# Second expert layer of a fused attention and mixture-of-experts kernel: loop order of the four row tiles and the three split terms

## The chip, the cores and the metric

The kernel runs on one core of a Trainium2 chip. The metric is device time in microseconds (us) of the whole launch; the time before is a median of three runs. One more execution was taken with the hardware profiler, and every statement on where time goes comes from that one.

TensorE multiplies a stationary operand (128 x 128, loaded by its own weight-load instruction) with a moving operand and adds the result into a region of PSUM, the accumulator memory. ScalarE (ACT), VectorE (DVE) and GpSimd (POOL) work beside it, each from its own queue in order; SyncE (SP) issues most DMA transfers.

## The reference

Two stages in fp32. The first is an attention over channels, for each of 4 batches of 5056 tokens with 256 channels; the second sends each of the 20224 resulting rows through one of 8 experts, chosen by the largest gate logit.

```python
qn = q / (norm(q, axis=1) + 1e-6); kn = k / (norm(k, axis=1) + 1e-6)
a = softmax(kn.T @ qn / tau)              # 256 x 256 per batch
x = (v @ a).reshape(20224, 256)
logits = x @ w_gate + modality_bias[modality_id]
e = argmax(logits); gate_w = softmax(logits)[e]
out = gate_w * (relu(x @ w1[e]) @ w2[e])  # w1[e]: 256 x 1024, w2[e]: 1024 x 256
```

## The kernel before, in words

**Split products.** TensorE's fp32r form is used for speed, and each operand is split into a high part (rounded to fp32r) and a low part (the rest). A product of two fp32 matrices then takes three terms: high times high, high times low, low times high. In names, `h` at the end is the high part and `l` the low one: `w2h`, `w2l`, `hh`, `hl`.

**Stages.** A first stretch builds the 256 x 256 Gram matrices (`g`, L343) of the batches from `q` and `k`, 512 tokens a step. After a softmax, `v` is transposed (`vtp`, L521), multiplied with the attention and gate weights (`xp`, L539), routed, and its rows are scattered by expert into a DRAM buffer `xs`. As soon as 512 rows of one expert stand there, a block can run. There are 40 blocks: 38 of four row tiles of 128 rows, and the last two of three tiles. Work on later batches (`g`, `vtp`, `xp`) is interleaved with the blocks until about 1080 us; after that only blocks remain.

**One block** (`block_pieces`). SP loads the expert's weights and the rows; ACT and DVE split the weights (L722, L729) and TensorE transposes the rows. For each of eight slices j of the 1024 hidden units:

- `m1(j)`: six products of 512 columns (384 in a three-tile block) into one PSUM tile `hp`; then ACT makes `hh` = relu (L765) and DVE `hl`, what is left of it (L766).
- `m2(j)`: the second layer. For each row tile t, three products of 256 columns each into the tile's accumulator region: `hh*w2h`, `hh*w2l`, `hl*w2h`. The stationary operand is the slice of `hh` or `hl` for row tile t, the moving one 256 columns of `w2h` or `w2l`. Twelve products a slice, 96 a block of four tiles.

The four accumulator regions lie in two PSUM tiles: `y0` holds row tiles 0 and 1, `y1` holds 2 and 3. There is one copy of each, so the next block can write them only when they have been read. After the eighth slice, `finish(t)` lets ACT copy region t, scaled with the gate weight, to `yo` (L796), and POOL scatters those rows to the output (L454).

**Order.** `m2(j)` is emitted two slices behind `m1(j)`. Around the end of a block the order is: first layer slice 0 of the next block, `m2(6)`, first layer slice 1 of the next, `m2(7)`, the four copies, first layer slice 2 of the next, then `m2(0)` of the next, which writes `y0` and `y1` again. A scheduler in the tile layer puts the emitted instructions into the engines' queues and may move ready ones ahead; on the chip each queue runs in the order in which it then stands. A reader of PSUM waits for the last write to the tile (here `y0` or `y1`), not to a region of it. In the last block the last three slices are emitted one row tile at a time.

Of the kernel before, what the change touches and what calls it, by code (L numbers as in the profile page):

```python
# [34 lines left out]
def kernel(  # L35
# [14 lines left out]
    P = 128  # L50
# [390 lines left out]
    def order(ins, others):  # L441

        for other in others:
            tc.add_manual_dep(
                ins, other.name,
                mybir.DependencyInfo(mybir.DependencyClass.NoSync, mybir.DependencyReason.DATA),
                reason="order on a queue",
            )
# [224 lines left out]
    def block_pieces(g, slot, picked, tail):  # L673
        pki, padded = picked
        st = {"wr": {}, "wc": {}, "h": {}}
# [95 lines left out]
        def m2(j, ts=range(tt)):  # L771
            if j == 0:
                st["y"] = [ps1.tile([P, 2, D], F32, tag=f"y{i}", name=f"y{i}_{slot}") for i in range(2)]
            _, _, w2h, w2l = st["wc"][j // 2]
            hh, hl = st["h"][j]
            for t in ts:
                y = st["y"][t // 2][:, t % 2, :]
                tsl = slice(t * P, (t + 1) * P)
                for i, (a, w) in enumerate(((hh, w2h), (hh, w2l), (hl, w2h))):
                    ins = nc.tensor.matmul(  # L780
                        y, a[:, tsl], w[:, j % 2, :],
                        start=(j == 0 and i == 0 and t % 2 == 0), stop=(j == NJ - 1 and i == 2),
                        skip_group_check=True,
                    ).ins
                    if slot == NB_MIN - 1 and j >= NJ - 3:

                        if t > 0:
                            order(ins, st["prev"][t - 1])
                        st.setdefault("prev", {}).setdefault(t, []).append(ins)
# [23 lines left out]
        for j in range(1, NJ):  # L813
            body.append(lambda j=j: m1(j))
            if j % 2 == 1 and (j + 1) // 2 + 1 < NJ // 2:
                body.append(lambda j=j: split_w((j + 1) // 2 + 1))
            if j >= BEHIND and (not ending or j - BEHIND < NJ - 3):
                body.append(lambda j=j: m2(j - BEHIND))
        if ending:

            last = []
            for t in range(tt):
                last += [lambda j=j, t=t: m2(j, range(t, t + 1)) for j in range(NJ - 3, NJ)]
                last.append(lambda t=t: finish(t))
        else:
            last = [lambda j=j: m2(j) for j in range(NJ - BEHIND, NJ)]
            last += [lambda t=t: finish(t) for t in range(tt)]
# [170 lines left out]
```

## Time and profile before

| what | value |
|---|---|
| median of three runs | 1247.93 us (1247.73 to 1249.01) |
| the profiled execution | 1241.93 us, span 1240.2 us |
| granted TensorE clock | 0.997 |
| TensorE matmuls | 1215.5 us busy, 98% of the span, 8368 |
| of these, second layer (L780) | 3 x 1264 products |
| VectorE / ScalarE / GpSimd busy | 67% / 59% / 29% |

In a row of the profile `y<-w2h,hh` means: writes `y`, reads moving `w2h` and stationary `hh`. `x1264` is a count, and after the bar come the busy time in us and the mean of one in ns. The busy time of one product is the time from its start to its end; successive products overlap, so the step from one start to the next is shorter than that.

### The profile page before, as it was taken

Reading aid. Unit: us, or ns where it says so; the run is one execution under the profiler, and the core shown is the slowest. Engines: PE = TensorE matmul, PEld = TensorE weight load, DVE = VectorE, ACT = ScalarE, POOL = GpSimd, SP = SyncE. Lnnn points to the kernel's source line nnn. Section 1 sums busy time; section 2 is a strip of 40 time slices with the busy share of each in tenths; the row PEclk is TensorE's granted clock in tenths of the full one; section 3 lists DMA queues with packets and bytes.
Section 4 is the critical chain, followed back from the end, with each engine's and each line's share of the span. In section 5 each row is a group of like instructions: output and inputs, shape, how many; then the busy total and the mean of one; then the engine's idle time right before and its main releaser. Section 6 shows DMA issues by size and latency. Waiting matters only on the chain. (4 is left out here: it accounts for less than half of the span.)

```text
span 1240.2 us, 23781 instructions
## 1 busy us (share of the span) xinstructions
PE 1215.5 (98%) x8368; PEld 1116.8 (90%) x8368; DVE 829.3 (67%) x2182; ACT 736.7 (59%) x1511; POOL 365.1 (29%) x344
## 2 busy tenths in 40 slices
PE   8989999999999999999999999999999999999997
PEld 7878898999999999998999999999899999989997
DVE  6789687767667776776677776656555665575552
ACT  6656667766666666675666666556455555545552
POOL 0053342223232333312333323322322233333121
PEclk9999999999999999999999999999999999999999
DMA  8979565455555565545555554444554454443430
GB/s 309 297 236 298 161 200 174 156 171 177 185 184 171 172 182 184 178 143 165 178 181 188 154 185 152 147 131 138 174 165 137 148 162 149 126 145 123 147 98 29
DMA packets 104177, 210.83 MB, mean 170 GB/s; under 512 B 11336, under 2 KB 52808, under 8 KB 104048
## 3 DMA queue, kind: packets, MB, share of 16 engines
q1 hardware_dynamic: 88304, 167.61, 43.5%
q0 software_dynamic: 15744, 41.61, 9.0%
q8 instruction: 67, 1.10, 0.4%
q14 instruction: 62, 0.51, 0.1%
HBM read 167.06 MB, written 43.43 MB: 170 GB/s over the span
## 5 line engine op out<-in xcount | busy, mean ns | idle before, releaser
L454 POOL DMA_INDIRECT xs<-x,pi x160 | 179.5, 1122 | 681.5 <-ACT w1h L722 302.3
L780 PE MATMUL y<-w2h,hh 128*128 128x256 f32 x1264 | 357.6, 283 | 1.8 <-issue 0.9
L780 PE MATMUL y<-w2l,hh 128*128 128x256 f32 x1264 | 352.6, 279 | 0.1
L780 PE MATMUL y<-w2h,hl 128*128 128x256 f32 x1264 | 350.9, 278 | 0.1
L766 DVE SCALAR_TENSOR_TENSOR hl<-hp,hh 128x512 fp32r<-128x512 f32 (+1 forms) x320 | 216.4, 676 | 67.8 <-ACT hh L765 61.4
L762 PE MATMUL hp<-xh,w1h 128*128 128x512 f32 (+1 forms) x640 | 254.4, 398 | 0.0
L762 PE MATMUL hp<-xh,w1l 128*128 128x512 f32 (+1 forms) x640 | 250.3, 391 | 0.0
L762 PE MATMUL hp<-xl,w1h 128*128 128x512 f32 (+1 forms) x640 | 249.9, 391 | 0.0
L780 PEld LDWEIGHTS y<-w2h,hh 128*128 128x128 f32 x1264 | 237.5, 188 | 13.1 <-ACT yo L796 1.9
L780 PEld LDWEIGHTS y<-w2l,hh 128*128 128x128 f32 x1264 | 238.0, 188 | 10.1 <-issue 0.5
L765 ACT ACTIVATE hh<-hp 128x512 fp32r<-128x512 f32 (+1 forms) x320 | 190.3, 595 | 82.6 <-PE hp L762 75.7
L780 PEld LDWEIGHTS y<-w2h,hl 128*128 128x128 f32 x1264 | 236.7, 187 | 0.5 <-DVE hl L766 0.3
L729 DVE TENSOR_TENSOR w1l<-w1r,w1h 128x512 fp32r<-128x512 f32 x160 | 110.2, 689 | 179.4 <-ACT w1h L722 171.3
L454 POOL DMA_INDIRECT out_dram<-yo,xr x158 | 171.7, 1087 | 158.0 <-ACT yo L796 121.4
L722 ACT CAST w1h<-w1r 128x512 fp32r<-128x512 f32 x160 | 100.1, 626 | 142.9 <-PE hp L762 130.1
L762 PEld LDWEIGHTS hp<-xh,w1l 128*128 128x128 f32 x640 | 120.1, 188 | 26.0
L762 PEld LDWEIGHTS hp<-xl,w1h 128*128 128x128 f32 x640 | 120.4, 188 | 14.7 <-issue 0.4
L762 PEld LDWEIGHTS hp<-xh,w1h 128*128 128x128 f32 x640 | 120.1, 188 | 12.7
L722 ACT CAST w2h<-w2r 128x512 fp32r<-128x512 f32 x160 | 101.0, 631 | 48.4 <-PE y L780 45.8
L729 DVE TENSOR_TENSOR w2l<-w2r,w2h 128x512 fp32r<-128x512 f32 x160 | 110.2, 689 | 25.3 <-ACT w2h L722 23.2
L543 ACT COPY x<-xp 128x264 f32<-128x264 f32 x160 | 61.2, 383 | 91.2 <-PE xp L539 67.5
L539 PE MATMUL xp<-ah,vh 128*128 128x264 f32 x320 | 93.1, 291 | 0.4 <-issue 0.4
(146 smaller groups left out, 1710.4 us busy)
## 6 DMA issues: line engine op xcount, KB each, us to landing
w1r<-in_moe_w_dram SPq DMA_DIRECT2D x80, 512.0 KB
w2r<-in_moe_w_dram SPq DMA_DIRECT2D x80, 512.0 KB
xr<-xs SPq DMA_DIRECT2D x38, 516.0 KB
v<-in_v_dram SPq DMA_DIRECT2D x36, 512.0 KB
q<-in_q_dram SPq DMA_DIRECT2D x35, 512.0 KB
k<-in_k_dram SPq DMA_DIRECT2D x35, 512.0 KB
xs<-x,pi POOLq DMA_INDIRECT x160
out_dram<-yo,xr POOLq DMA_INDIRECT x158
```

Of the source, the lines that this page charges most:

```text
L454: ins = nc.gpsimd.indirect_dma_start(out=dst, out_offset=bass.IndirectOffsetOnAxis(ap=idx, axis=0), in_=rows, in_offset=None, bounds_check ...
L539: nc.tensor.matmul(xp[:, 0:DE], a[:, h, t * P : (t + 1) * P], w[:, h, :], start=i == 0, stop=i == len(seq) - 1,)
L543: nc.scalar.copy(st["x"][:, t, :], xp[:, 0:DE])
L722: ins = nc.scalar.copy(hi, src).ins
L729: nc.vector.tensor_tensor(lo, src, hi.bitcast(F32), ALU.subtract)
L762: nc.tensor.matmul(hp[:, 0:rows], w[:, h, fs], x[:, h, 0:rows], start=i == 0, stop=i == len(seq) - 1)
L765: nc.scalar.activation(hh[:, 0:rows], hp[:, 0:rows], AF.Relu)
L766: nc.vector.scalar_tensor_tensor(hl[:, 0:rows], hp[:, 0:rows], 0.0, hh[:, 0:rows].bitcast(F32), ALU.max, ALU.subtract)
L780: ins = nc.tensor.matmul(y, a[:, tsl], w[:, j % 2, :], start=(j == 0 and i == 0 and t % 2 == 0), stop=(j == NJ - 1 and i == 2), skip_group ...
```

## The change

In `m2` the loop over the three terms goes outside, and the loop over the row tiles inside. The same twelve products are issued, with the same operands and into the same four regions. Before, three successive products went to one region. Now each goes to another region than the one ahead of it: `hh*w2h` for tiles 0, 1, 2, 3, then `hh*w2l` for all four, then `hl*w2h` for all four. The start flag (first slice, first term, tiles 0 and 2) and the stop flag are those of before. Where `m2` is called for a single tile (the last three slices of the last block) the order stays. Line numbers behind L780 move up by two; L780 is L778 in the changed kernel, L796 is L794.

```diff
-            for t in ts:
-                y = st["y"][t // 2][:, t % 2, :]
-                tsl = slice(t * P, (t + 1) * P)
-                for i, (a, w) in enumerate(((hh, w2h), (hh, w2l), (hl, w2h))):
+            for i, (a, w) in enumerate(((hh, w2h), (hh, w2l), (hl, w2h))):
+                for t in ts:
                     ins = nc.tensor.matmul(
-                        y, a[:, tsl], w[:, j % 2, :],
+                        st["y"][t // 2][:, t % 2, :], a[:, t * P : (t + 1) * P], w[:, j % 2, :],
                         start=(j == 0 and i == 0 and t % 2 == 0), stop=(j == NJ - 1 and i == 2),
                         skip_group_check=True,
                     ).ins
```

TensorE's queue, last slice of block 35 (`y0_35` and `y1_35` are its two accumulator tiles). Before:

```order
L780 MATMUL y0_35_16314<-w2h_35_3_16343,hh_35_7_16467 128x256 [waits Activation_49]
L780 MATMUL y0_35_16314<-w2l_35_3_16344,hh_35_7_16467 128x256
L780 MATMUL y0_35_16314<-w2h_35_3_16343,hl_35_7_16468 128x256
L780 MATMUL y0_35_16314<-w2h_35_3_16343,hh_35_7_16467 128x256
L780 MATMUL y0_35_16314<-w2l_35_3_16344,hh_35_7_16467 128x256
L780 MATMUL y0_35_16314<-w2h_35_3_16343,hl_35_7_16468 128x256
L780 MATMUL y1_35_16315<-w2h_35_3_16343,hh_35_7_16467 128x256
```

Five more rows on `y1` follow it. In the changed kernel the slice reads:

```order
L778 MATMUL y0_35_16314<-w2h_35_3_16343,hh_35_7_16467 128x256 [waits Activation_49]
L778 MATMUL y0_35_16314<-w2h_35_3_16343,hh_35_7_16467 128x256
L778 MATMUL y1_35_16315<-w2h_35_3_16343,hh_35_7_16467 128x256 x2
L778 MATMUL y0_35_16314<-w2l_35_3_16344,hh_35_7_16467 128x256 x2
L778 MATMUL y1_35_16315<-w2l_35_3_16344,hh_35_7_16467 128x256 x2
L778 MATMUL y0_35_16314<-w2h_35_3_16343,hl_35_7_16468 128x256 x2
L778 MATMUL y1_35_16315<-w2h_35_3_16343,hl_35_7_16468 128x256 x2
```

The last write to `y0` was the sixth product of the slice and is now the tenth; that to `y1` stays the twelfth. The first write to `y1`, which in the next block's first slice waits for ACT's copies, was the seventh and is now the third.

ACT's queue at the end of block 4, one of those in the mixed stretch, as a difference:

```order
 L765 ACTIVATE hh_5_1_3632<-hp_5_1_3625 128x512
-L796 ACTIVATE yo_4_3652<-y0_4_3259,xr_4_2608 128x256 x2
-L796 ACTIVATE yo_4_3652<-y1_4_3260,xr_4_2608 128x256 x2
+L322 ACTIVATE sq_2_3_0_k_4552<-k_2_3_4505 128x512
+L794 ACTIVATE yo_4_3652<-y0_4_3259,xr_4_2608 128x256 x2
 L525 CAST vh_12_3621<-vtp_12_0_3657 128x512
+L794 ACTIVATE yo_4_3652<-y1_4_3260,xr_4_2608 128x256 x2
 L525 CAST vh_12_3621<-vtp_12_1_3688 128x512
 L722 CAST w2h_5_3_3751<-w2r_5_1_3089 128x512
-L322 ACTIVATE sq_2_3_0_k_4552<-k_2_3_4505 128x512
```

The scheduler puts a square (`sq`) ahead of the copies and a cast of `vh` between the two pairs of copies. In the stretch with blocks alone (block 35, for one) ACT's order is unchanged.

## The prediction

> **What bounds the kernel now.** I read the page's busy times first, then the stretches, then the waits. The question was whether TensorE waits for anybody or is itself the limit.
>
> ```profile
> span 1240.2 us, 23781 instructions
> PE 1215.5 (98%) x8368; PEld 1116.8 (90%) x8368; DVE 829.3 (67%) x2182; ACT 736.7 (59%) x1511; POOL 365.1 (29%) x344
> L780 PE MATMUL y<-w2h,hh 128*128 128x256 f32 x1264 | 357.6, 283 | 1.8 <-issue 0.9
> L780 PE MATMUL y<-w2l,hh 128*128 128x256 f32 x1264 | 352.6, 279 | 0.1
> L780 PE MATMUL y<-w2h,hl 128*128 128x256 f32 x1264 | 350.9, 278 | 0.1
> ```
>
> TensorE is busy for 98% of the span, the next engine for 67%. The second layer is 3792 products, and the idle time ahead of its three rows is 1.8, 0.1 and 0.1 us. Only two things can therefore move the time: how fast TensorE steps from product to product, and new waits. The stretches and TensorE's waits, from the views that group them:
>
> ```profile
> 600.00:900.00 300.00, 299.42 (x2108) 276.43 (x2107) 199.66 (x523) 178.41 (x366) 91.09 (x84) 1.00 0.51 160
> 1080.00:1232.00 152.00, 151.13 (x1027) 140.35 (x1026) 82.33 (x195) 75.43 (x151) 42.97 (x42) 1.00 0.35 110
> PE y L780 <- ACT yo L796: 0.8, 2, 0.6
> PEld y L780 <- ACT yo L796: 1.9, 3, 0.8
> PEld y L780 <- DVE hl L766: 0.3, 1, 0.3
> ```
>
> TensorE is full both in the mixed stretch (299.42 of 300 us) and in the one with blocks alone (151.13 of 152), at a granted clock of 1.00, so the clock has no room to rise. The waits of the second layer are on ACT's copies `yo`, 0.8 us and 1.9 us, and 0.3 us on `hl`. The chain of waits is of no help here: it ends on POOL and "issue" and names no TensorE work.
>
> **The change part by part. First part: the step.** Nothing is added: 3792 products and as many weight loads stay. What may change is the step. These are starts on TensorE in the last slice of block 35 and around it, ACT's four copies, and below them durations over the whole run (minimum, median, maximum):
>
> ```profile
> 1152.34 0.28 PE L780 MATMUL y<-w2h,hh 128*128 128x256 f32 x1
> ...
> 1152.94 0.28 PE L780 MATMUL y<-w2h,hl 128*128 128x256 f32 x1
> 1153.06 0.28 PE L780 MATMUL y<-w2h,hh 128*128 128x256 f32 x1
> ...
> 1153.40 0.28 PE L780 MATMUL y<-w2h,hh 128*128 128x256 f32 x1
> 1153.52 0.28 PE L780 MATMUL y<-w2l,hh 128*128 128x256 f32 x1
> 1153.64 0.27 PE L780 MATMUL y<-w2h,hl 128*128 128x256 f32 x1
> 1153.75 0.39 PE L762 MATMUL hp<-xh,w1h 128*128 128x512 f32 x1
> ...
> 1155.13 0.28 PE L780 MATMUL y<-w2h,hh 128*128 128x256 f32 x1
> ...
> 1155.36 0.28 PE L780 MATMUL y<-w2h,hl 128*128 128x256 f32 x1
> ```
>
> ```profile
> L780 PE MATMUL y<-w2h,hh x1264: 277/279/388, 99.6 to 1232.1; 128*128 128x256 f32 x181
> L780 PE MATMUL y<-w2l,hh x1264: 277/277/387, 99.8 to 1232.2; 128*128 128x256 f32 x181
> L780 PE MATMUL y<-w2h,hl x1264: 274/276/386, 102.7 to 1232.4; 128*128 128x256 f32 x181
> L796 ACT ACTIVATE yo<-y,xr x158: 459/476/513, 129.2 to 1232.7; 128x256 f32<-128x256 f32 x158
> ```
>
> ```profile
> 1153.33 1.56 ACT L796 ACTIVATE yo<-y,xr 128x256 f32<-128x256 f32 x4
> ```
>
> The twelve products take 1153.75 - 1152.34 = 1.41 us, 117.5 ns each. A duration of 279 ns holds that step and about 160 ns in which the next product already runs, so I read differences of durations as differences of steps. By the medians, `hh*w2h` is the slowest (279), then `hh*w2l` (277), then `hl*w2h` (276); by the means 283, 279, 278.
>
> The fast one is the last of its row tile: the product behind it goes to another region. The two slower ones are followed by a product into the region that they have just written. There is a cleaner comparison: during `hl*w2h` of one tile and `hh*w2h` of the next, TensorE streams the same `w2h` and loads the same weights, `hh` of the next tile, for the product behind it. They differ in the part held in the array, in whether the successor uses the same moving operand, and in whether it writes the same region. Now every product inside a term has a successor with the same moving operand and another region, like the fast row. So the nearest row says that all three settle at the third row's value: by medians (279-276) + (277-276) = 4 ns per row tile and slice, times 1264 = 5.1 us; by means (283-278) + (279-278) = 6 ns, 7.6 us. The mean of the first row holds a few waits, so I take 6 us between the two.
>
> The bounds of this term: all three at the least that the third row shows, 274: (5 + 3 + 2) x 1264 = 12.6 us saved. On the other side stands the Gram row, where successive products also change region, after every third one:
>
> ```profile
> L343 PE MATMUL g<-qs,ks 128*128 128x256 f32 (+1 forms) x600 | 81.8, 283 | 1.3 <-issue 1.3
> ```
>
> These are split products of 256 columns too, and they average 283 ns. If all second-layer products went to 283, against 283 + 279 + 278 = 840 now, 9 ns x 1264 = 11.4 us would be added. I take the value near the first end because it comes from the same operands.
>
> **Second part: the copies at the block's end.** In the rows above, `y0` is last written by the sixth product (1152.94, ends 1153.22), and ACT starts its four copies at 1153.33, 0.11 us later. It runs them back to back and ends at 1153.33 + 1.56 = 1154.89. Now the last write to `y0` is the tenth product, four steps later: 4 x 0.1175 = 0.47 us. The copies start near 1153.80 and end near 1155.36. The next block's first slice starts at 1155.13. Before, `y1` was wanted by its seventh product, now by its third, at 1155.36, with the weight load some 0.1 us ahead of that. So here TensorE waits some 0.15 us where it waited for nothing. Behind the copies in ACT's queue stand the cast of `w2h` and relu of the next first-layer slice; they too come up to 0.47 us late, but that relu's `hh` is wanted only after four more slices of about 1.4 us, which hide it.
>
> With a three-tile block behind, the first layer between is shorter:
>
> ```profile
> 1198.43 1.56 ACT L796 ACTIVATE yo<-y,xr 128x256 f32<-128x256 f32 x4
> 1199.96 0.28 PE L780 MATMUL y<-w2h,hh 128*128 128x256 f32 x1
> ...
> 1200.19 0.28 PE L780 MATMUL y<-w2h,hl 128*128 128x256 f32 x1
> ```
>
> Copies would end at 1199.99 + 0.47 = 1200.46, and `y1` is wanted at 1200.19 less 0.1: 0.35 to 0.4 us. By the timeline, only the first layer's six products stand between at eight of the 39 block ends: six like block 35 (6 x 0.15 = 0.9 us) and two with a three-tile block (2 x 0.4 = 0.8 us). Two more have ACT late already, as here, where TensorE waited for `y0`:
>
> ```profile
> 1108.99 0.39 PE L780 MATMUL y<-w2h,hh 128*128 128x256 f32 x1 [0.21 <-ACT yo L796]
> ```
>
> There `y1` comes four steps sooner, 2 x 0.4 = 0.8 us. The other 29 have transposes or `xp` products between, which cover the copies and the cast that the scheduler puts among them:
>
> ```profile
> 684.14 1.03 PE L521 MATMUL vtp<-ident,v 128*128 128x128 f32 x8
> 684.93 0.48 PE L762 MATMUL hp<-xh,w1h 128*128 128x512 f32 x1
> ```
>
> The transposes give 684.93 - 684.14 = 0.8 us more. Were that cover gone, each end could cost the full 0.47 us, 29 x 0.47 = 13.6 us. Bounds of this part: 0, and 2.5 + 13.6 = 16.1 us; I take 0.9 + 0.8 + 0.8 = 2.5 us.
>
> **Third part.** `hl` is wanted as the ninth product instead of the third, which can save the 0.3 us in the row above and no more. The last three slices of the last block stand as they stood, so the end of the kernel, with POOL's stores, is unchanged.
>
> **Sum:** -6 + 2.5 - 0.3 = -3.8 us. The profiled execution took 1241.93 us around its span of 1240.2, and the median is 6.0 us above that. I carry the difference over to the median: 1247.93 - 3.8 = **1244.1 us**.
>
> **The rivals.** Changes under 0.2%, 2.5 us, cannot be told from none.
>
> *The step does not depend on the region.* Then only the waits are left: 1247.93 + 2.2 = 1250.1 us. For it: the Gram row changes region every third product and is no faster; the order 279, 277, 276 may belong to the operands themselves. Against it: the comparison above, in which streamed and loaded operands are the same.
>
> A rule for this rival, by itself: the Trainium skill, "TensorE: Matmul & The Clock Gate", section "Back-to-back issue gap", gives the step at full clock as N/2.4 + 2.5 ns, an estimate of 109 ns for 256 columns, with no term for the accumulator. The trace has 117.5 ns, so something that the rule leaves out costs time here, and the rule does not say whether the change touches it. By that rule the first part would be nothing.
>
> *The step gets longer,* to the Gram row's mean: +11.4 + 2.2 gives 1261.5 us. For it: fresh weights at every product, where before the second of three loaded the slice that the array already held. Against it: the weight loads are as many as before, and the third row, which is followed by fresh weights, is the fast one.
>
> *The copies turn into a wait at every block end.* One mechanism: four products later on ACT, four sooner on TensorE. It decides once the last copy ends later than 0.23 us behind the first product of the next block. With the gain on the step kept this is 1247.93 - 6 + 16.1 = 1258.0 us. For it: the rows of blocks 35 and 37 are already there. Against it: 0.8 us of transposes or the like at most other ends.
>
> **How the numbers follow.** Forecast 0.42, with a range of its own from 1236 to 1248; step unchanged 0.28; step longer 0.18; copies everywhere 0.12. Faster by over 0.2%: nine tenths of the forecast and a little of the second case, 0.40. Within 0.2%: the rest of the forecast, about 0.04, most of the second case, 0.20, and 0.03 from mild forms of the others: 0.27. Slower: 0.33. The range reaches from 1236, the first bound less the waits (1247.93 - 12.6 + 0.5), to 1258, where the copies' case stands and about half of the longer-step case is left out.
>
> **What would show it.** If the step depends on the region, the L778 rows all fall to 276 ns or less and to nearly one value, and a slice takes under 1.39 us; if the operands decide it, the order 279, 277, 276 stays; if fresh weights cost, the first two rows rise above 280. The copies should start four steps later in block 35, and the wait of `y` for `yo` should rise from 0.8 + 1.9 us by some 2.5 us; 10 us or more there would mean the last rival. The forecast is wrong if TensorE's busy time does not fall by about 6 us.

## The result and the profile after

The changed kernel takes 1264.15 us, the median of four runs (1263.23 to 1266.07), against 1248.46 us for four runs of the kernel before on the same chip. The ratio is 1.0124, with a 95% interval of 1.011 to 1.0137: 15.7 us slower. Forecast were 1244.1 us and a range of 1236 to 1258. In two later sets of runs the ratio was 1.0159 and 1.0174. The profiled execution of the changed kernel has a span of 1262.5 us, 22.3 us more than before.

The changed kernel's page, its groups and its waits (the numbers in a row of waits are us in all, times, and the longest one in us):

```profile
span 1262.5 us, 23777 instructions
PE 1227.7 (97%) x8368; PEld 1126.0 (89%) x8368; DVE 832.5 (66%) x2182; ACT 736.7 (58%) x1511; POOL 359.3 (28%) x344
L778 PE MATMUL y<-w2h,hh 128*128 128x256 f32 x1264 | 211.6, 285 | 13.8 <-ACT yo L794 13.4 <-issue 0.2
L778 PE MATMUL y<-w2h,hl 128*128 128x256 f32 x1264 | 203.4, 282 | 0.1
L778 PE MATMUL y<-w2l,hh 128*128 128x256 f32 x1264 | 202.1, 279 | 0.0
PEld y L778 <- ACT yo L794: 18.7, 20, 2.6
PE y L778 <- ACT yo L794: 13.4, 15, 2.2
ACT sq_k L322 <- DMA k<-in_k_dram: 21.5, 17, 3.5
```

Two things differ. The second layer's wait for the copies `yo` rose from 0.8 to 13.4 us on the products and from 1.9 to 18.7 us on their weight loads; the two overlap, so they are not added. And `hl*w2h`, before the fastest of the three groups (278 ns), now averages 282 ns. The busy times of these rows (211.6 us where the first had 357.6) cannot be held against those of before: time in which products of one row overlap counts once, and now four of a row stand together.

Where the time goes is seen by stretches. Busy time of TensorE is the first pair behind the length, the granted clock the number behind the five pairs. Before, and then after:

```profile
300.00:400.00 100.00, 100.00 (x710) 92.61 (x709) 67.68 (x166) 61.48 (x125) 27.16 (x24) 1.00 0.50 162
```

```profile
300.00:400.00 100.00, 96.28 (x652) 88.13 (x651) 64.92 (x153) 58.70 (x119) 30.17 (x27) 0.97 0.50 161
600.00:900.00 300.00, 298.31 (x2089) 275.17 (x2089) 199.70 (x519) 177.95 (x364) 88.01 (x82) 1.00 0.51 161
```

Between 300 and 400 us TensorE issued 652 matmuls instead of 710, and its clock fell to 0.97. By the start of the last second-layer product of a block, the changed kernel is behind by 3.0 us at block 3 (227.86 against 230.81), by 13.2 us at block 7 (349.59 against 362.83), and by 22.3 us at block 38. So 3.0 us are lost up to block 3, 10.2 us in four blocks, and 9.1 us over the 31 behind them. Of the 3.0 us, 1.6 stand there already at the first second-layer product (101.24 against 99.62 us), ahead of all that the change touches. Of the 10.2 us, TensorE's waits for the copies of blocks 4, 5 and 6 make 0.71, 2.59 and 2.88 us, a lower clock 3.4 us and the step (both below) 0.4 us. Of the 9.1 us, the step makes 31 x 96 x 1.07 ns = 3.2 us and waits for copies at seven ends 4.9 us, where the kernel before has 0.2.

This is what happens in the four blocks. ACT at the end of block 6, first in the kernel before, then in the changed one; in brackets stands the idle time ahead of the row and what ended it:

```profile
318.93 0.59 ACT L765 ACTIVATE hh<-hp 128x512 fp32r<-128x512 f32 x1
319.42 1.56 ACT L796 ACTIVATE yo<-y,xr 128x256 f32<-128x256 f32 x4
320.85 1.10 ACT L525 CAST vh<-vtp 128x512 fp32r<-128x512 f32 x2
...
323.42 0.63 ACT L322 ACTIVATE sq_k<-k 128x512 f32<-128x512 f32 x1 [0.96 <-DMA k<-in_k_dram]
```

```profile
325.96 0.59 ACT L765 ACTIVATE hh<-hp 128x512 fp32r<-128x512 f32 x1
330.07 0.63 ACT L322 ACTIVATE sq_k<-k 128x512 f32<-128x512 f32 x1 [3.51 <-DMA k<-in_k_dram]
330.60 0.82 ACT L794 ACTIVATE yo<-y,xr 128x256 f32<-128x256 f32 x2
331.32 0.58 ACT L525 CAST vh<-vtp 128x512 fp32r<-128x512 f32 x1
331.78 0.86 ACT L794 ACTIVATE yo<-y,xr 128x256 f32<-128x256 f32 x2
```

ACT's waits for loads of `k` ahead of such squares are 21.5 us in all in the changed kernel; before they were:

```profile
ACT sq_k L322 <- DMA k<-in_k_dram: 15.7, 15, 3.3
```

Here the square of `k` waits for a load, and starts 4 to 4.5 us behind relu in both kernels (330.07 - 325.96 and 323.42 - 318.93). Before, the four copies ran in that time. Now the square stands ahead of them in ACT's queue, ACT idles 3.51 us with the copies behind it, and a cast parts the two pairs. TensorE at the same place:

```profile
326.40 0.63 PE L778 MATMUL y<-w2h,hl 128*128 128x256 f32 x4
...
328.91 0.40 PE L762 MATMUL hp<-xh,w1l 128*128 128x512 f32 x1
331.48 0.51 PE L778 MATMUL y<-w2h,hh 128*128 128x256 f32 x2 [2.17 <-ACT yo L794]
332.69 0.80 PE L778 MATMUL y<-w2h,hh 128*128 128x256 f32 x2 [0.71 <-ACT yo L794]
333.29 1.05 PE L778 MATMUL y<-w2l,hh 128*128 128x256 f32 x4
334.14 1.05 PE L778 MATMUL y<-w2h,hl 128*128 128x256 f32 x4
```

It waits 2.17 us for `y0`, runs two products, and waits again, 0.71 us, for `y1`. Behind that the four `w2l` products take 334.14 - 333.29 = 0.85 us instead of 0.47: the clock is down, as the stretches show (granted clock behind the five pairs).

```profile
328.00:331.00 3.00, 1.31 (x6) 0.73 (x4) 0.27 (x1) 0.93 (x3) 0.00 (x0) 1.00 0.69 217
331.00:332.00 1.00, 0.51 (x2) 0.30 (x2) 0.49 (x2) 1.00 (x4) 0.67 (x1) 0.94 0.13 53
334.00:335.00 1.00, 1.00 (x7) 1.00 (x7) 1.00 (x3) 1.00 (x3) 1.00 (x1) 0.50 0.38 131
336.00:340.00 4.00, 4.00 (x20) 3.48 (x19) 0.90 (x3) 1.50 (x3) 1.10 (x1) 0.66 0.56 192
```

The granted clock falls to 0.50 just before 332 us and is back near 338.7 (4 us at a mean of 0.66). At half speed for 6.8 us TensorE does 3.4 us less work, which is more than the wait itself.

### The profile page after: what moved, and what is told of

Read it like the earlier page. It is cut to its first block, busy times and chain, and to the rows that moved or that the text cites. A ratio compares the mean times of both kernels' runs of the same rounds, so it can differ in the third digit from the quotient of the medians.

```text
span 1262.5 us, 23777 instructions
## 1 busy us (share of the span) xinstructions
PE 1227.7 (97%) x8368; PEld 1126.0 (89%) x8368; DVE 832.5 (66%) x2182; ACT 736.7 (58%) x1511; POOL 359.3 (28%) x344
## 4 chain that ended last, share of the span: by engine, by line
PE 80%; issue 7%; DMA 4%; ACT 4%; DVE 3%; POOL 1%; POOLq 0%; SPq 0%; ACTq 0%; DVEq 0%
PE y L778 30%; PE hp L762 28%; PE xp L539 9%; PE g L343 9%; DMA k<-in_k_dram 4%; PE vtp L521 2%; PE xtp L743 2%; ACT yo L794 1%; POOL out_dram L454 1%; DMA xs<-x,pi 1%; POOL xs L454 0%; ACT hh L765 0%; PE ns L370 0%; ACT vh L525 0%; DVE qs L299 0%
## 5 line engine op out<-in xcount | busy, mean ns | idle before, releaser
L778 PE MATMUL y<-w2h,hh 128*128 128x256 f32 x1264 | 211.6, 285 | 13.8 <-ACT yo L794 13.4
L778 PEld LDWEIGHTS y<-w2h,hh 128*128 128x128 f32 x1264 | 189.7, 188 | 39.3 <-ACT yo L794 18.7
L778 PE MATMUL y<-w2h,hl 128*128 128x256 f32 x1264 | 203.4, 282 | 0.1
L778 PE MATMUL y<-w2l,hh 128*128 128x256 f32 x1264 | 202.1, 279 | 0.0
L778 PEld LDWEIGHTS y<-w2l,hh 128*128 128x128 f32 x1264 | 172.3, 188 | 0.0
L778 PEld LDWEIGHTS y<-w2h,hl 128*128 128x128 f32 x1264 | 171.2, 188 | 0.3 <-DVE hl L766 0.3
```

The lines of the kernel that those rows point to most:

```text
L778: ins = nc.tensor.matmul(st["y"][t // 2][:, t % 2, :], a[:, t * P : (t + 1) * P], w[:, j % 2, :], start=(j == 0 and i == 0 and t % 2 == 0) ...
```

## The experiments

Ratios are to the kernel before on the same chip, in the same set of runs; its medians there lay between 1233 and 1245 us. "The step" is the mean time from the start of one second-layer product to the next matmul's start, in one profiled execution, over the 3660 to 3740 steps below 135 ns; the waits in the last column are of that one execution, too. The step is 116.88 ns before and 117.95 ns after. Times 3791 steps that difference of 1.07 ns is 4.1 us.

| kernel | ratio, 95% interval | step, ns | wait of `y` products for `yo`, us |
|---|---|---|---|
| change, again | 1.0159 (1.0124 to 1.0193) | 117.96 | 11.2 |
| change, a third time | 1.0174 (1.0143 to 1.0205) | 117.92 | 10.3 |
| slices 1 to 6 only | 1.0016 (1.0000 to 1.0032) | 117.72 | 0.6 |
| last slice only | 1.0070 (1.0044 to 1.0096) | 116.88 | 6.3 |
| first slice only | 1.0003 (0.9992 to 1.0014) | 117.04 | 1.2 |
| first and last slice | 1.0145 (1.0124 to 1.0167) | 117.03 | 11.9 |
| change, ACT's old queue | 1.0023 (1.0005 to 1.0042) | 117.91 | 1.4 |
| before, ACT's new queue | 1.0055 (1.0033 to 1.0078) | 116.90 | 6.7 |
| before, five squares ahead | 1.0036 (1.0019 to 1.0053) | 116.87 | 4.4 |
| change, five squares behind | 1.0080 (1.0054 to 1.0106) | 117.89 | 3.5 |
| regions turn | 0.9991 (0.9974 to 1.0008) | 116.86 | 0.6 |
| operands turn | 1.0015 (1.0000 to 1.0030) | 117.70 | 1.5 |
| fresh weights | 0.9997 (0.9979 to 1.0015) | 116.86 | 0.8 |
| snake | 1.0004 (0.9987 to 1.0021) | 117.71 | 0.6 |
| spread | 0.9998 (0.9987 to 1.0008) | 116.85 | 0.6 |

### Which slices: the middle, and the last

The slice's twelve products are put into one list, and the change's order is taken in some slices alone. For slices 1 to 6:

```diff
+            by_term = [(i, t) for i in range(3) for t in ts]
+            by_tile = [(i, t) for t in ts for i in range(3)]
+            todo = by_term if 0 < j < NJ - 1 else by_tile
+            for i, t in todo:
```

> Terms outside only in the second-layer slices 1 to 6 of a block; the first and the last slice as before. ACT's, DVE's, SP's and POOL's queues then stand exactly as before, and only TensorE's order differs, on 6/8 of the products. If the loss came from TensorE's step alone, 6/8 of the 15.7 us show: about +12 us. If ACT's queue and the late copies are the cause, only the small rise of the step is left, read as 1.05 ns on 3791 products (116.89 to 117.94 ns) = 4.0 us in all, 6/8 of it: +3 us.

Measured: 1.0016, 2.0 us. The queues of ACT, DVE, GpSimd and SyncE are those of the kernel before, the waits for `yo` stay at their old size, and the step is 117.72 ns. So the step's part can be had alone. The time's interval just reaches no change (1.0000); that it is a loss is read from the step.

For the last slice alone the condition is `j == NJ - 1`; the queues are then exactly those of the changed kernel.

> Terms outside only in the last slice of a block, 1/8 of the products. ACT's, DVE's, SP's and POOL's queues then stand exactly as in the changed kernel. If the step is the cause: +2 us (1/8 of 15.7). If the queues and the late copies are: 15.7 less 7/8 of the step's 4.0 us, about +12 us, and waits of y for yo near the changed kernel's 13.4 us.

Measured: 1.0070, 8.9 us, at the old step of 116.88 ns: nearer to the 12 us of the second theory than to the 2 us of the first, but short of it, with 6.3 us of waits where 13.4 were named. In its trace the loss arises in blocks 3 to 8: it is 0.7 us behind the kernel before at block 2, 11.6 at block 8 and 11.5 at the end. Not all of that is waits for the copies: 3.4 us are a clock at half for 6.8 us from 218 us on, behind a wait of 3.2 us for the routing (`rp`, L575), and in three kernels that lose nothing (first slice, fresh weights, spread) the clock fell there, too, for 3.4 us. The move of `y0`'s last write by four products, with all that the scheduler makes of it, is a large part of the loss.

### ACT's queue apart from the order of the products

Every instruction of ACT is tied, without a semaphore, behind the one that stands ahead of it in the other kernel's queue (its rows then carry the line of the recording helper, L134):

```diff
+    queue = [f"I-{n}" for n in ACT_QUEUE if f"I-{n}" in acts]
+    for one, two in zip(queue, queue[1:]):
+        tc.add_manual_dep(
+            acts[two], one,
+            mybir.DependencyInfo(mybir.DependencyClass.NoSync, mybir.DependencyReason.DATA),
+            reason="order on a queue",
+        )
```

First the changed kernel with the old queue:

> The whole change, but ACT's instructions tied to the order in which they stood before (each one behind the one ahead of it there, without a semaphore). If the squares and casts that the scheduler put ahead of the copies are the cause, the waits of y for yo fall from 13.4 us to about 2 or 3 and the kernel stands at +4 to +6 us (step 4.0 us, the copies four products later some 2 us). If the four products' delay of the copies is itself the cause, whatever stands in ACT's queue: still +12 us or more. DVE's queue moves a little too, which both leave at nothing.

Measured: 1.0023, 3.6 us, a little under the 4 to 6 expected. The changed products cost little once the copies stand in their old place, although they still start four products later than before. ACT at the end of block 6, and the row of the waits:

```profile
321.39 0.60 ACT L134 ACTIVATE hh<-hp 128x512 fp32r<-128x512 f32 x1
322.26 1.57 ACT L134 ACTIVATE yo<-y,xr 128x256 f32<-128x256 f32 x4 [0.28 <-PE y L868]
```

```profile
PEld y L868 <- ACT yo L134: 2.7, 5, 0.9
```

The copies follow relu again and are released by TensorE itself (0.28 us of idle time behind relu); the weight loads of `y` wait 2.7 us in all (1.9 before), and the 3.6 us are about the step's 4.1. VectorE's queue was not tied: in this kernel and the three others whose ACT queue is set, it differs at some places from both kernels', and what that is worth was not measured.

Then the kernel before, products in the old order, with the changed kernel's queue:

> TensorE's products in the order before, but ACT's instructions tied to the order of the changed kernel. If ACT's queue order is the cause: +8 to +12 us without any change of a loop, with ACT waiting for a load of k ahead of the copies of blocks 4 to 6. If it needs the late copies as well: within 2 us of before.

Measured: 1.0055, 6.9 us, under the 8 to 12 us expected and well over the rival's 2 us, with every second-layer slice in its old order (elsewhere a few products of `g` and transposes trade places) and the step at 116.90 ns. At the end of block 6 ACT shows the same picture as in the changed kernel: 3.00 us of waiting for `k`, and the copies behind it. The queue's order is a cause by itself.

```profile
327.45 0.63 ACT L134 ACTIVATE sq_k<-k 128x512 f32<-128x512 f32 x1 [3.00 <-DMA k<-in_k_dram]
```

### Squares or casts

At 40 block ends the two queues differ in few things: five squares of `q` or `k` (blocks 1, 2, 4, 5, 6) and fourteen casts of `w1h` stand ahead of the copies instead of behind, and at 28 block ends a cast of `vh` stands among them. For the next two kernels only the five squares are moved, in the list that sets ACT's queue; at block 6, with names in place of the list's instruction numbers:

```diff
+sq_k (block 6; k still loading)
 yo   (block 6, four copies)
 vh, vh, w2h
-sq_k
```

The changed kernel itself ran beside them as a mark:

> The changed kernel as it is, on the chip of the next three, as their upper mark. Both theories: about 1.012 of the time before, +15 us. If the parts add (ACT's queue order with the old product order +6.9 us, the change with ACT's old queue order +3.6 us), some 4 us of it come only when both are there: the later copies behind the later queue.

Measured: 1.0159, 20.8 us, above the 15 us expected. The parts (6.9 and 3.6, from the set of runs before) come to 10.5, so of the 15.7 to 20.8 us some 5 to 10 appear only when both are there.

> The kernel before, products in the old order; of ACT's queue only five squares (blocks 1, 2, 4, 5, 6) are put ahead of the block's four copies, where the changed kernel has them; the casts stay behind the copies. Theory 'a square that waits for its load holds up the copies': +5 to +7 us, ratio about 1.005, y waits for yo by 6 us or more, the loss comes at the ends of blocks 4, 5 and 6 (1.5 to 3.5 us each). Rival 'the casts of vh between the copies and of w1h ahead of them, some 0.6 us at 25 block ends': under +1.5 us, ratio under 1.0015.

Measured: 1.0036, 4.8 us, from five instructions that were moved ahead. Block 6 again, first ACT, then TensorE, then the stretch behind the wait:

```profile
329.54 0.63 ACT L134 ACTIVATE sq_k<-k 128x512 f32<-128x512 f32 x1 [3.32 <-DMA k<-in_k_dram]
330.08 1.55 ACT L134 ACTIVATE yo<-y,xr 128x256 f32<-128x256 f32 x4
```

```profile
330.95 0.42 PE L870 MATMUL y<-w2h,hh 128*128 128x256 f32 x1 [1.97 <-ACT yo L134]
```

```profile
332.00:334.00 2.00, 2.00 (x12) 2.00 (x11) 1.87 (x4) 2.00 (x6) 1.60 (x2) 0.50 0.37 131
```

ACT waits 3.32 us, TensorE 1.97 us, and the half clock (0.50) follows. The expected 6 us of waits were 4.4 us on the products and 6.8 on their weight loads; the ratio lies a little under the 1.005 expected and outside what the casts alone were given (1.0015).

> The changed kernel; of ACT's queue only the same five squares are put back behind the copies, the casts stay where the change has them. Theory 'squares': falls to about the changed kernel with the whole old queue, +3.5 to +6 us against the kernel before, y's wait for yo under 5 us. Rival 'casts': stays within 3 us of the changed kernel, +12 us or more.

Measured: 1.0080, 9.8 us. Putting the squares back takes 11 us off the changed kernel beside it (1.0159 - 1.0080), about half of its loss; by the two intervals it could be 5 to 15 us. But 9.8 us stay where 3.5 to 6 were expected: neither theory is enough. With the whole old queue it was 3.6 us. The casts are all that differs in ACT's queue between these two kernels, so by subtraction some 6 us are theirs; no kernel moves the casts alone. In the changed kernel's own trace the waits behind block 6, 4.9 us at seven ends, stand where none of the five squares does. The profiled execution of this kernel was its fastest (1249.74 us), so the remainder is seen there in part only.

### Why the parts do not add: the first slice

> The change's product order in slice 0 of a block alone: the next block wants y1 by its third product instead of its seventh, while the copies start as before and ACT's queue keeps its old order. By the prediction's sum the block ends with only the first layer between lose nothing here (the copies end 0.24 us before the next slice starts, and y1's weights are wanted later than that); only the two ends where ACT is late and the two with a three-tile block could lose 0.4 us each: +0.5 to +1.5 us, no change within 0.2%. Rival 'y1 sooner is a wait of its own': +3 us or more.

Measured: 1.0003, no change, as expected. `y1` wanted four products sooner costs nothing while the copies are early.

The change's order in slices 0 and 7, with the queues of the changed kernel:

> The change's product order in slices 0 and 7 of a block alone, with the queues of the changed kernel; slices 1 to 6 as before. If the last slice gives +9 us through the queue, the first nothing by itself but some 4 us on top of late copies, this gives +12 to +13 us, and with the 3 us of slices 1 to 6 the changed kernel's +16. If the first slice adds nothing even then: +9 us, and 4 us of the changed kernel stay without a cause.

Measured: 1.0145, 19.4 us between the medians, at a step of 117.03 ns: more than either theory had (9, or 12 to 13 us), and most of the changed kernel's loss in that set of runs. The first slice alone had 0.03% there, the last alone 0.70% in an earlier set: together they cost about twice what they cost apart. The trace is of the slowest of five executions. TensorE at the end of block 6, first with the last slice alone, then with both:

```profile
332.33 0.39 PE L783 MATMUL y<-w2h,hh 128*128 128x256 f32 x1 [1.24 <-ACT yo L799]
333.03 0.28 PE L783 MATMUL y<-w2h,hl 128*128 128x256 f32 x1
333.55 0.39 PE L783 MATMUL y<-w2h,hh 128*128 128x256 f32 x1 [0.24 <-ACT yo L799]
```

```profile
328.12 0.51 PE L783 MATMUL y<-w2h,hh 128*128 128x256 f32 x2 [1.89 <-ACT yo L799]
329.34 0.80 PE L783 MATMUL y<-w2h,hh 128*128 128x256 f32 x2 [0.71 <-ACT yo L799]
329.93 1.05 PE L783 MATMUL y<-w2l,hh 128*128 128x256 f32 x4
```

Once the copies are late, TensorE waits first for `y0` and then for `y1`, whose copies come a cast and two copies later. With six products on `y0` in hand (332.33 to 333.03) it covers most of that second wait, and 0.24 us is left; with two it does not, and 0.71 us is left. By starts, the third product comes 329.34 - 328.12 = 1.22 us behind the first, where 0.23 us would be free of waits.

> The changed kernel on the chip of the two runs before this one, as their upper mark: ratio 1.012 to 1.016, +15 to +20 us.

Measured: 1.0174, 23.7 us between the medians, a little above what was expected. The difference from both ends, 0.29%, is about what slices 1 to 6 add by their step; but the two intervals overlap, so this sum is not exact.

### The step: region or operands

Five kernels change slices 1 to 6 alone; the queues of ACT, DVE, GpSimd and SyncE have the rows of the kernel before. First the region without the operand order, then the operand order without the region:

```diff
+            inner = 0 < j < NJ - 1
+            todo = by_tile if inner else by_tile
+            for n, (i, t) in enumerate(todo):
+                r = ts[n % len(ts)] if inner else t
...
-                        y, a[:, tsl], w[:, j % 2, :],
+                        st["y"][r // 2][:, r % 2, :], a[:, t * P : (t + 1) * P], w[:, j % 2, :],
```

> The kernel before in its old operand order; in slices 1 to 6 of a block each product is added to the region behind that of the product before it (0, 1, 2, 3, 0, ...), so the output is not the reference's: a row tile's terms are spread over the four regions. First, last slice and all queues as before. Theory of the prediction (a new region makes the step shorter): the mean step of y falls from 116.9 ns by 1 ns or more, -3 us. Theory 'a new region costs': it rises to 117.7 ns as in the changed kernel, +2 us. Theory 'the region does not matter, the operand order does': 116.9 ns stays, no change within 0.2%.

```diff
+            todo = by_term if inner else by_tile
+            for n, (i, t) in enumerate(todo):
+                r = ts[n // 3] if inner else t
```

> The counterpart of the kernel in which only the regions turn: in slices 1 to 6 the operands come in the change's order (one term for four row tiles, then the next), but three successive products are added to one region as before, so the output is not the reference's: the regions hold other rows' terms. Queues as before. Theory 'the operand order makes the step longer, the region does not matter': mean step of y 117.6 to 117.9 ns in the trace, +2 us, ratio 1.001 to 1.003. Rival 'only both together do': 116.9 ns, no change.

The duration of `hl*w2h` (minimum, median, maximum) in the one and in the other:

```profile
L785 PE MATMUL y<-w2h,hl x1264: 274/276/385, 102.5 to 1234.2; 128*128 128x256 f32 x181
```

```profile
L785 PE MATMUL y<-w2h,hl x1264: 274/281/415, 103.0 to 1236.4; 128*128 128x256 f32 x181
```

With a new region at every product the step stays (116.86 ns, 0.9991) and `hl*w2h` keeps its 276 ns. With the old regions and the new operand order the step is 117.70 ns, `hl*w2h` has 281 ns as in the changed kernel, and the ratio is 1.0015. The region does not matter to the step; the operand order does.

What in that order? Three properties go together in it: fresh weights at every product, one moving operand for four products in a row, and four `hl` products in a row at the end of the slice.

```diff
+            two = ((0, 0), (1, 1), (2, 0), (1, 0), (0, 1), (2, 1))
+            pairs = [(i, p + u) for p in range(0, len(ts) - 1, 2) for i, u in two]
+            fresh = pairs + by_tile[len(pairs):]
```

> In slices 1 to 6 of the kernel before, two row tiles a and b are interleaved so that no product has the stationary operand of the one before it (hh of a, hh of b, hl of a, hh of a, hh of b, hl of b); the moving operand stays the same from one product to the next in 5 of 12 steps of a slice or fewer, as before, not in nine. Queues as before. Theory 'a newly loaded stationary operand at every product costs the nanosecond': mean step of y 117.6 ns or more, +2 us. Rival 'four products in a row on one moving operand cost it': 116.9 ns, no change within 0.2%.

```diff
+            snake = [(i, t) for t in ts for i in ((0, 1), (1, 0))[t % 2]] + [(2, t) for t in ts]
```

> In slices 1 to 6 of the kernel before the terms run to and fro: hh of tile 0 with w2h, w2l, hh of tile 1 with w2l, w2h, and so on, then hl of the four tiles with w2h. The stationary operand repeats in 4 of 12 steps as before; the moving one repeats in some eight steps instead of three. Queues as before. Theory 'newly loaded stationary operands cost': 116.9 ns or slightly less, no change. Theory 'repeated moving operands cost': 117.5 ns or more, +2 us. If both the repeats save something, the step falls below 116.5 ns and the time by 1.5 us.

Fresh weights at every product cost nothing: 116.86 ns, 0.9997. The snake keeps the weights' repeats and has 117.71 ns, though its time (1.0004) shows no loss. In its slices the moving operand repeats in 7 of the 11 steps (3 before, 9 in the change), as that theory asks, but it also has the four `hl` in a row. So one more kernel parts these two: the `hh` products in the change's order, and one `hl` at every third place. There the moving operand repeats in 7 of 11 steps as well.

```diff
+            high = [(i, t) for i in range(2) for t in ts]
+            spread = [x for t in ts for x in (*high[2 * t : 2 * t + 2], (2, t))]
```

> In slices 1 to 6 of the kernel before the eight products with hh run in the change's order (w2h for the four row tiles, then w2l), each into another region than the one before, but the four products with hl are not bunched at the end: one stands at every third place, as before. Queues as before. Theory 'the four hl products one behind the other make the step longer': mean step of y back at 116.9 ns, no change within 0.2%. Rival 'the order of the hh products, terms outside, does it': 117.5 ns or more, +2 us.

```profile
L785 PE MATMUL y<-w2h,hl x1264: 274/276/415, 100.8 to 1225.4; 128*128 128x256 f32 x181
```

The step is back at 116.85 ns, the median of `hl*w2h` at 276, the ratio at 0.9998. Every kernel with `hl` bunched at the end of slices 1 to 6 has the longer step (117.70 to 117.96 ns), and every one with one `hl` in three there the old one (116.85 to 117.04). From the starts, a step that begins with an `hl` product is 115.1 ns on the mean before (1257 steps) and 118.6 ns after (1256); those of the two `hh` terms go from 118.9 to 118.0 and from 116.8 to 117.3. Parted by what stands ahead: in the changed kernel an `hl` product behind an `hh` product steps in 114.3 ns (322 steps), one behind another `hl` product in 120.1 ns (934). Why is not shown by any run. The times of these kernels alone could hardly tell 2 us from nothing; the step, read over 3700 records, does.

## Why the prediction was wrong, point by point

**What bounds the kernel.** Right: TensorE was full, and the time moved by its step, by new waits, and by a clock that fell behind them. The prediction asked only whether the clock could rise.

**First part, the step (-6 us).** Wrong in sign. The step that failed is the reading "the fast one is the last of its row tile: the product behind it goes to another region". The fast row was fast for its place in a sequence of operands. Turning the regions alone moved nothing, and the order in which that fast row was put together with its like made it the slowest: +1.07 ns a step, +4.1 us, and 0.16% in slices 1 to 6. The comparison "in which streamed and loaded operands are the same" had named two other differences and then gone by the third. The named test did tell: the `L778` medians became 280, 279 and 281, not 276, and TensorE's busy time rose from 1215.5 to 1227.7 us where it was to fall by 6.

**Second part, the copies (+2.5 us).** The priced mechanism was right, and small. ACT and then TensorE in the changed kernel, at the end of block 35:

```profile
1175.49 1.57 ACT L794 ACTIVATE yo<-y,xr 128x256 f32<-128x256 f32 x4 [0.28 <-PE y L778]
```

```profile
1176.91 0.71 PE L778 MATMUL y<-w2h,hh 128*128 128x256 f32 x4
1177.45 0.63 PE L778 MATMUL y<-w2l,hh 128*128 128x256 f32 x4
```

0.54 us to the next term instead of 0.47: a wait of 0.07 us where 0.15 was forecast. The copies came 0.38 us later, not 0.47: before, they had started right behind relu (0.49 us behind its start, now 1175.49 - 1174.62 = 0.87), so 0.09 us of the delay was time in which ACT was not free anyway. With ACT's old queue, where little but this delay is left, the products wait 1.4 us in all against 0.8 before, 0.6 us where the sum had 2.5, and the whole changed kernel costs 3.6 us, step included.

The step that failed is "the other 29 have transposes or `xp` products between, which cover the copies and the cast that the scheduler puts among them". The cover was held against a delay of four products, 0.47 us. But ACT's queue had changed: the square of `k` stood ahead of the copies in the quoted rows of block 4, and its own wait for the load of `k` (15.7 us in all in the profile before, where the copies stood ahead of it) was not added. At block 6 that wait is 3.51 us against a cover of 0.8 us. Five squares alone make 4.8 us; in the change, taking them back saves about 11 us. One reason stands in the rows: the first slice then waits twice. The upper bound of 16.1 us was about the size of the loss, but was reached by long waits at few block ends and a lower clock behind one of them, not by 0.47 us at each.

**Third part, `hl` (-0.3 us).** The wait for `hl` stays at 0.3 us; nothing was saved. In both traces it stands in the last slices of the last block (at 1229.3 us before), whose order the change leaves as it was.

**The rivals.** "The step does not depend on the region" was right on the region, and wrong in that nothing would follow. By itself: the Trainium skill, "TensorE: Matmul & The Clock Gate", section "Back-to-back issue gap", whose rule has no term for the accumulator, agrees with the turned regions (116.86 ns). The section gives its 109 ns for 256 columns, an estimate, as the gap of an isolated product, without the weight loads of this kernel; the measured 116.9 to 118 ns differ from it, and the order of the operands, worth 1 ns here, is not in it. "The step gets longer" came nearest in time, with 1261.5 us, but for the wrong reason: its term was almost three times too large (11.4 against 4.1 us), its cause, fresh weights, costs nothing, and most of the loss is not in the step. "The copies turn into a wait at every block end", with 1258.0 us, had the right place for the larger part, and its sign, waits of 10 us or more, came; but at most ends the copies stayed covered (the stretch from 600 to 900 us has 298.31 us of work), and what made them late at the others was the queue, not the four products.

**The missing term.** The half clock behind a wait of 2 us was in no part of the sum. At block 6 it is 3.4 us behind waits of 2.17 and 0.71 us.

## What to carry to other kernels

When a change moves what one engine waits for, read the other engines' queues in their new order, and for each instruction that now stands ahead of a critical one ask what it waits for itself; its idle time in the old profile, where nobody stood behind it, is the price. A shift that is free by itself (accumulator wanted sooner, 0.03%) can double the price of another (copies later, 0.70% alone, 1.45% together), so hold their sum against the cover. And before a difference of 3 ns between rows is given a cause, vary the candidates one at a time: several properties changed together with this order, and the one that was taken for the cause had no effect.

## What was not expected of the hardware

**The clock falls after short waits, but not after each.** Behind waits of TensorE of 1.97 and 2.17 us the granted clock went from 1.00 to 0.50; with the first (five squares ahead) it was low for about 3.4 us (three windows of 2 us at 0.79, 0.50 and 0.86, which is 1.7 us of lost clock), with the second for about 6.8 us. The length of the wait does not decide it. In the same execution of the changed kernel, waits of 1.87 and 0.72 us a block earlier left the clock at 1.00:

```profile
298.12 0.50 PE L778 MATMUL y<-w2h,hh 128*128 128x256 f32 x2 [1.87 <-ACT yo L794]
299.33 0.50 PE L778 MATMUL y<-w2h,hh 128*128 128x256 f32 x2 [0.72 <-ACT yo L794]
300.00:304.00 4.00, 4.00 (x30) 3.75 (x29) 3.53 (x7) 3.20 (x7) 3.12 (x3) 1.00 0.46 125
```

In the changed kernel's third profiled execution, waits of 0.90 and 0.72 us brought it to 0.50:

```profile
261.12 0.50 PE L778 MATMUL y<-w2h,hh 128*128 128x256 f32 x2 [0.90 <-ACT yo L794]
262.34 0.50 PE L778 MATMUL y<-w2h,hh 128*128 128x256 f32 x2 [0.72 <-ACT yo L794]
264.00:266.00 2.00, 2.00 (x9) 1.89 (x9) 1.89 (x4) 1.20 (x3) 1.70 (x2) 0.50 0.28 48
```

There the clock fell behind three block ends in a row, at 263.21, 297.34 and 331.47 us by the trace's clock records, for 3.41 us each; the spacing of 34.13 us is ten times that length. A wait of 1.24 us at the end of block 6, with the last slice alone, left the clock at 1.00:

```profile
332.00:334.00 2.00, 1.43 (x9) 1.23 (x10) 0.96 (x2) 2.00 (x6) 1.51 (x2) 1.00 0.58 229
```

The Trainium skill, "TensorE: Matmul & The Clock Gate", "What's actually happening", puts the fall behind an idle window of about 3.4 us that runs freely. The lengths at half clock and the spacing agree with such windows; the waits that sufficed here are shorter than one. So what a short wait costs depends on when it comes, and one profiled execution has its share of luck in it.

**The step knows the order of its operands, not its region.** Between the same twelve products in two orders lies 1 ns of 117, tied to four `hl` products in a row (120.1 ns behind another `hl`, 114.3 behind an `hh`). What in the hardware does this is open.
